# Loading FFN weights by column parts, halving a projection pass and turning held weight pieces on VectorE, in a fused kernel of memory attention and FFN

## The chip, the cores and the metric

The kernel runs on one core of a Trainium2 chip. The metric is the device time of one launch in microseconds. A time is the median over runs; the traces are of single executions.

## The reference

The input x has 2048 rows of 640. Attention goes through it in 64 segments of 32 rows; each segment sees 8 memory rows and its own rows, and its output for the memory rows is the next segment's memory. A feed-forward network (FFN) works on the same x, and a gate mixes the two.

```python
mem = mem0
for s in range(n_seg):                       # 64, one after the other
    xs = x[:, s * seg_len:(s + 1) * seg_len, :]
    h = jnp.concatenate([mem, xs], axis=1)   # 8 + 32 rows
    q = jnp.einsum('btd,dhe->bhte', h, Wq)   # 32 heads of 192; k and v alike
    ...
    scores = jnp.einsum('bhqe,bhke->bhqk', q, k) * scale
    scores = jnp.where(mask[None, None], scores, -1000000000.0)
    p = _softmax(scores, axis=-1)
    o = jnp.einsum('bhqk,bhke->bhqe', p, v)
    o = jnp.einsum('bhte,hed->btd', o, Wo)
    mem = o[:, :M, :].copy()
    outs.append(o[:, M:, :])
a = jnp.concatenate(outs, axis=1)
b = jnp.einsum('bsf,fd->bsd', _gelu(x @ w_gate) * (x @ w_up), w_down)   # 1536 inner columns
return g * a + (1 - g) * b                   # g = sigmoid((x * gate_w).sum(-1))
```

## The kernel before

The program is written as a list of operations. `_Sched.add` appends each to the stream of its engine and notes which regions of SBUF, PSUM and HBM it reads and writes; semaphore waits follow from these regions. Within an engine the order is the order of the calls, and a DMA belongs to the stream of the engine that issues it: SP issues the loads of weights and x, ACT the stores and the loads of scratch data (`AUXQ`). A wait stands in the stream, so it holds back all that comes behind it. Two operations that write one region keep their order, even when they touch different parts of it.

The work has three stages.

1. The FFN (`ffn_transposes`, `ffn_gu`, `ffn_down`), in four blocks of 512 rows. For each of 12 groups f of 128 inner columns, TensorE computes G (L782) and U (L785), each from five 128-row slices; ACT applies gelu (L788) and VectorE multiplies (L790). SP loads x's first block, `w_gate`, `w_up` (each 1920 KB in one DMA), x's second block and `w_down`, then pieces of the attention's weights.

2. The left pass (L844 to L871). "Left" names the 8 rows of every segment that don't fit beside the memory rows in a 32-row tile: 64 segments of 8, 512 columns (`XL`). Their Q and K need no memory, so they are computed ahead for all segments. An octant `o_` is 8 heads; for each of four octants and for Q and K there are 12 chunks of 128 output columns, each five matmuls of 128x512 (L852) into one PSUM bank, banks 0 to 7 in turn. Chunks are evicted by VectorE (L862) and ACT (L859) in turn, into one of two staging areas `lst`, and both name the whole area as the region they write. At the octant's end ACT issues four stores of 768 KB to HBM scratch (L867).

3. The segments (`segment`), by the hand-written order `PROG`: for each octant Q, K (`cmode`, L931; evicted L935), V and left V (L951), scores (L993), softmax, weighted sums (L1071), then Wo (L1094). VectorE copies the segment's memory rows (L1139), from which the next segment starts. Left Q/K of the segment come from scratch with `stg_load` (L907), left x with `xleft_load`.

The attention's weights are cut into 108 pieces of 384 or 320 KB. Most are resident in SBUF, 20 are streamed for every segment through a ring of five slots (L567), and two are held in unused parts of PSUM: `HELD2` (a piece of Wq) and `HELD` (a piece of Wo), which ACT copies to SBUF in each segment (`held2_copy`, L610, and `held_copy`, L623). Residents have three classes by their place. Class 0 is loaded at the start; class 2, above the staging areas, after the FFN (`load_residents(2)`); class 1, under `XL` and the staging areas, only when the left pass is done (`load_late`), at most `LATE` = 24 pieces ahead of use. The left pass needs streamed pieces too (`issue_left`, L635, through the same ring).

Between left pass and segments, `chain_init` transposes the first memory on TensorE (L728), ACT issues `x_load(0)` (L678), and ACT evicts the transposed memory into the same tile behind it (L732). `held_init` then brings the two held pieces into PSUM so that ACT's later copy is plain data: it loads a piece, transposes it by 128x128 blocks on TensorE (L882), copies it to SBUF on VectorE (L885) and transposes it back into its PSUM places (L896), first `HELD2`, then `HELD` through the same buffers.

Of the kernel before, what the change touches and what calls it, by code (L numbers as in the profile page):

```python
# [3 lines left out]
ACTF = mybir.ActivationFunctionType  # L4
# [217 lines left out]
def _build(nc, A_x, A_mem0, A_Wq, A_Wk, A_Wv, A_Wo, seg_len, w_gate, w_up, w_down,  # L222
           gate_w, out, opts=None):
    opts = dict(opts or {})
    Bsz, S, Dm = A_x.shape
    M = A_mem0.shape[1]
# [112 lines left out]
    def bview(o, nbytes, plo=0, phi=128):  # L339
        return arena[plo:phi, o // 2:(o + nbytes) // 2]  # L340
# [4 lines left out]
    def sreg(o, nbytes, plo=0, phi=128):  # L345
        return Rg("sb", o, o + nbytes, plo, phi)
# [71 lines left out]

    wg_sb = bview(ffn_off["wg"], KT * Df * 2).rearrange("p (k f) -> p k f", f=Df)
    wu_sb = bview(ffn_off["wu"], KT * Df * 2).rearrange("p (k f) -> p k f", f=Df)  # L420
    wd_sb = bview(ffn_off["wd"], FT * Dm * 2).rearrange("p (f n) -> p f n", n=Dm)
    r_wg = sreg(ffn_off["wg"], KT * Df * 2)
    r_wu = sreg(ffn_off["wu"], KT * Df * 2)
    r_wd = sreg(ffn_off["wd"], FT * Dm * 2)
# [12 lines left out]
    XLB = KT * NL * 2  # L437
    STB = NSEG * 2 * LW * 2
    o_XL = ffn_base - XLB
# [8 lines left out]
    def psb(bank):  # L448
        return ps[:, bank, :].bitcast(BF)
# [17 lines left out]
    def piece_size(key):  # L467
        return GO if key[0] == 3 else GQ
# [123 lines left out]
    late_done = [0]  # L592
    LATE = 24

# [55 lines left out]
    def load_residents(cls):  # L650
        for key in order:
            if key in res_off and slot_class[key] == cls:
                load_resident(key)
# [34 lines left out]
    ffn_x_load(0)  # L688
    S_.add("sp", lambda e: e.dma_start(wg_sb, w_gate.rearrange("(k p) f -> p k f", p=128)), writes=[r_wg], dma_sem="wg")
    S_.add("sp", lambda e: e.dma_start(wu_sb, w_up.rearrange("(k p) f -> p k f", p=128)), writes=[r_wu], dma_sem="wu")  # L690
    if NFB > 1:
# [33 lines left out]

    def chain_init():
        pv7 = psb(7)
        S_.add("pe", [lambda e, k=k: e.transpose(pv7[:, k * M:(k + 1) * M], mem0r[0:M, k * 128:(k + 1) * 128], ident[0:M, 0:M])  # L728
                      for k in range(KT)],
               reads=[r_mem0r, r_ident], writes=[r_ps[7]], name="mem0T")  # L730
        x_load(0)
        S_.add("act", lambda e: e.activation(out=Hb[0][:, :, 0:M], in_=pv7[:, 0:KT * M].rearrange("p (k m) -> p k m", m=M),  # L732
                                             func=ACTF.Copy),
               reads=[r_ps[7]], writes=[r_Hm[0]], name="mem0T evac")

# [43 lines left out]
    def ffn_gu(blk):  # L779
        for f in range(FT):  # L780
            gb = 3 + 2 * (f % 2)
            S_.add("pe", [lambda e, k=k, f=f, gb=gb: e.matmul(ps[:, gb, 0:FB].rearrange("p (s t) -> p s t", t=L), wg_sb[:, k, f * 128:(f + 1) * 128], xT_sb[:, k],  # L782
                                                              start=(k == 0), stop=(k == KT - 1)) for k in range(KT)],
                   reads=[r_wg] + r_xT, writes=[r_ps[gb]], name="ffn G %d %d" % (blk, f))
            S_.add("pe", [lambda e, k=k, f=f, gb=gb: e.matmul(ps[:, gb + 1, 0:FB].rearrange("p (s t) -> p s t", t=L), wu_sb[:, k, f * 128:(f + 1) * 128], xT_sb[:, k],  # L785
                                                              start=(k == 0), stop=(k == KT - 1)) for k in range(KT)],
                   reads=[r_wu] + r_xT, writes=[r_ps[gb + 1]], name="ffn U %d %d" % (blk, f))
            S_.add("act", lambda e, f=f, gb=gb: e.activation(out=gl_sb[f % 2], in_=ps[:, gb, 0:FB], func=ACTF.Gelu_apprx_tanh),  # L788
                   reads=[r_ps[gb]], writes=[r_gl[f % 2]], name="ffn gelu")
            S_.add("dve", lambda e, f=f, gb=gb: e.tensor_tensor(out=hT_sb[:, f, :], in0=ps[:, gb + 1, 0:FB], in1=gl_sb[f % 2], op=ALU.mult),  # L790
                   reads=[r_ps[gb + 1], r_gl[f % 2]], writes=[r_hT[f]], name="ffn h")
# [43 lines left out]
    S_.add("sp", lambda e: e.dma_start(mem0r[0:M, :], A_mem0[0]), writes=[r_mem0r], dma_sem="mem0")  # L835
    gate_spread()
    load_residents(2)
    for lo, hi in ((0, NG // 2), (NG // 2, NG)):
# [5 lines left out]
    for o_ in range(NOCT):  # L844
        st, rst_ = lst[o_ % 2], r_lst[o_ % 2]
        for m in range(2):
            gs = [left_piece((m, o_, k)) for k in range(KT)]
            for i in range(12):
                bk = nbk[0] % 8
                nbk[0] += 1  # L850
                c = i
                S_.add("pe", [lambda e, k=k, g_=gs[k][0], i=i, bk=bk: e.matmul(  # L852
                    ps[:, bk, 0:NL].rearrange("p (g t) -> p g t", t=L), g_[:, i * 128:(i + 1) * 128], XL[:, k], start=(k == 0), stop=(k == KT - 1))
                    for k in range(KT)], reads=[x[1] for x in gs] + [r_XL], writes=[r_ps[bk]],
                    name="left o%d m%d c%d" % (o_, m, i))
                dst = st[:, :, m].rearrange("p s (b r h) -> p s b r h", b=6, h=2)[:, :, c // 2, :, c % 2]
                src = ps[:, bk, 0:NL].rearrange("p (s i) -> p s i", i=M)
                if i % 2:
                    S_.add("act", lambda e, dst=dst, src=src: e.activation(out=dst, in_=src, func=ACTF.Copy),  # L859
                           reads=[r_ps[bk]], writes=[rst_], name="left evac")  # L860
                else:
                    S_.add("dve", lambda e, dst=dst, src=src: e.tensor_copy(out=dst, in_=src),  # L862
                           reads=[r_ps[bk]], writes=[rst_], name="left evac")
        nd = max(1, NSEG // 16)
        for d in range(nd):
            lo, hi = d * NSEG // nd, (d + 1) * NSEG // nd
            S_.add(AUXQ, lambda e, lo=lo, hi=hi, st=st, o_=o_: e.dma_start(  # L867
                qkl[lo:hi].rearrange("s p c -> p s c")[:, :, 2 * LW * o_:2 * LW * (o_ + 1)],
                st[:, lo:hi].rearrange("p s m c -> p s (m c)")),
                reads=[rst_], writes=[Rg("qk", 64 * o_ + lo, 64 * o_ + hi)], dma_sem="lst%d_%d" % (o_ % 2, d),  # L870
                name="left store")  # L871

    def held_init(key, parts):
        n = piece_size(key) // 2
        t1, r1 = bview(wsB_off["Q"], 2 * n), sreg(wsB_off["Q"], 2 * n)
        t2, r2 = bview(wsB_off["vl"], 2 * n), sreg(wsB_off["vl"], 2 * n)
        assert wsB_off["stg"] >= wsB_off["Q"] + 2 * n and n % 128 == 0
        dst = t1.rearrange("p (c n) -> p c n", n=Dm) if key[0] == 3 else t1
        S_.add("sp", lambda e: e.dma_start(dst, piece_src(key)), writes=[r1], dma_sem="held%d" % key[0], name="held load")
        for b, c0 in ((3, 0), (4, 8)):  # L880
            nb = min(8, n // 128 - c0)
            S_.add("pe", [lambda e, b=b, c=c, c0=c0: e.transpose(psb(b)[:, 128 * (c - c0):128 * (c - c0 + 1)],  # L882
                                                                 t1[:, 128 * c:128 * (c + 1)], ident)
                          for c in range(c0, c0 + nb)], reads=[r1, r_ident], writes=[r_ps[b]], name="heldT")
            S_.add("dve", lambda e, b=b, c0=c0, nb=nb: e.tensor_copy(out=t2[:, 128 * c0:128 * (c0 + nb)],  # L885
                                                                     in_=psb(b)[:, 0:128 * nb]),
                   reads=[r_ps[b]], writes=[r2], name="heldT evac")
        for b, c0, c1, p0 in parts:
            fns = []
            c = c0  # L890
            while c < c1:
                blk, lo = divmod(c, 128)
                hi = min(128, lo + c1 - c)
                if lo == 32:
                    hi = 64
                fns.append(lambda e, b=b, blk=blk, lo=lo, hi=hi, o=p0 + c - c0: e.transpose(  # L896
                    psb(b)[:, o:o + hi - lo], t2[lo:hi, 128 * blk:128 * (blk + 1)], ident[lo:hi, lo:hi]))
                c += hi - lo
            S_.add("pe", fns, reads=[r2, r_ident], writes=[r_ps[b]], name="heldTT")

    chain_init()
    issue_ring(0, B_RING - 1)
    held_init(HELD2, HB2)
    held_init(HELD, [(b, 256 * b, 256 * b + 256, 768) for b in range(5)])
    S_.add("pool", lambda e: e.memset(p_sb, 0.0), writes=[r_p])
# [352 lines left out]
```

## Time and profile before

| | |
|---|---|
| median of four runs | 1905.13 us (1892.21 to 1909.58) |
| the profiled execution | 1909.52 us, of which the span is 1907.7 |
| TensorE busy | 1757.6 us, 92% of the span |
| VectorE, ACT busy | 928.6 us (49%), 875.5 us (46%) |
| data moved | 550.98 MB, mean 289 GB/s |
| FFN | up to 183.15 us |
| left pass | 183.15 to 293.94 us |
| first scores | 325.93 us |
| end of segment 0 (L1139) | 354.38 us |
| mean granted TensorE clock | 0.983 |

Times in the profile are from the start of the span. A row of the timeline gives start, duration, engine, line, operation, output and input, number of instructions, and in brackets how long the engine had been idle and what released it. ACTq and SPq are the engines' sequencers while they issue DMAs. Busy time of TensorE contains pipelining, so a busy TensorE is not one at its peak.

### The profile page before, as it was taken

Reading aid. Unit: us, or ns where it says so; the run is one execution under the profiler, and the core shown is the slowest. Engines: PE = TensorE matmul, PEld = TensorE weight load, DVE = VectorE, ACT = ScalarE, POOL = GpSimd, SP = SyncE. Lnnn points to the kernel's source line nnn. Section 1 sums busy time; section 2 is a strip of 40 time slices with the busy share of each in tenths; the row PEclk is TensorE's granted clock in tenths of the full one; section 3 lists DMA queues with packets and bytes.
Section 4 is the critical chain, followed back from the end, with each engine's and each line's share of the span. In section 5 each row is a group of like instructions: output and inputs, shape, how many; then the busy total and the mean of one; then the engine's idle time right before and its main releaser. Section 6 shows DMA issues by size and latency. Waiting matters only on the chain.

```text
span 1907.7 us, 78857 instructions
## 1 busy us (share of the span) xinstructions
PE 1757.6 (92%) x34429; PEld 1128.2 (59%) x34429; DVE 928.6 (49%) x2890; ACT 875.5 (46%) x2045; POOL 145.1 (8%) x547
## 2 busy tenths in 40 slices
PE   7999995799999999999999999999999999899898
PEld 3454443566665666666666666666666566666565
DVE  3222322455555555555555555555555555555455
ACT  2222322355544554545555545454555554455444
POOL 1000000000000000000000100000000000000000
PEclk9999997999999999999999999999999999999999
DMA  9511567999999999999999999999999999999998
GB/s 372 197 35 33 151 171 226 331 317 306 312 312 310 318 317 297 329 313 324 313 323 316 338 309 325 299 328 306 325 313 332 305 323 310 311 316 310 296 313 272
DMA packets 280422, 550.98 MB, mean 289 GB/s; under 512 B 82434, under 2 KB 106506, under 8 KB 280074
## 3 DMA queue, kind: packets, MB, share of 16 engines
q1 hardware_dynamic: 201386, 506.45, 77.7%
q10 hardware_dynamic: 78688, 39.48, 7.5%
q8 instruction: 269, 4.41, 0.9%
q14 instruction: 79, 0.65, 0.1%
HBM read 524.69 MB, written 21.10 MB: 286 GB/s over the span
## 4 chain that ended last, share of the span: by engine, by line
PE 67%; DMA 23%; DVE 4%; ACTq 3%; ACT 1%; issue 1%; SPq 0%; DVEq 0%
PE ps L931 20%; DMA arena<-in_A_Wo_dram 13%; PE ps L951 11%; PE ps L1094 10%; PE ps L852 4%; PE ps L1071 4%; DMA arena<-in_A_Wv_dram 4%; DMA arena<-in_A_Wq_dram 3%; PE ps L993 3%; PE ps L785 3%; PE ps L782 3%; DMA arena<-in_A_Wk_dram 3%; ACTq L867 2%; PE ps L800 2%; PE ps L985 2%; PE ps L975 1%
## 5 line engine op out<-in xcount | busy, mean ns | idle before, releaser
L931 PE MATMUL ps<-arena 128*32 128x384 bf16 x10240 | 512.3, 332 | 32.9 <-DVE arena L1154 16.2
L1094 PE MATMUL ps<-arena 128*40 128x320 bf16 x6144 | 479.3, 299 | 38.2 <-DMA arena<-in_A_Wo_dram 34.1
L1094 PEld LDWEIGHTS ps<-arena 128*40 128x40 bf16 x6144 | 312.5, 99 | 139.2 <-DMA arena<-in_A_Wo_dram 69.2
L935 ACT ACTIVATE arena<-ps 128x384 bf16<-128x384 f32 x512 | 311.7, 609 | 148.1 <-PE ps L931 129.7
L931 PEld LDWEIGHTS ps<-arena 128*32 128x32 bf16 x10240 | 254.1, 97 | 174.9 <-DVE arena L1154 20.7
L951 PE MATMUL ps<-arena 128*32 128x384 bf16 x5800 | 294.3, 331 | 3.2 <-DMA arena<-in_A_Wv_dram 2.6
L941 DVE STREAM_TRANSPOSE arena<-arena 128x192 f32<-128x192 f32 x512 | 190.1, 371 | 118.5 <-ACT arena L935 118.2
L610 ACT ACTIVATE arena<-ps 128x576 bf16<-128x576 bf16 (+1 forms) x192 | 113.5, 591 | 243.1 <-PE ps L1094 240.1
L951 PEld LDWEIGHTS ps<-arena 128*32 128x32 bf16 x5800 | 147.3, 98 | 91.9 <-DMA arena<-in_A_Wv_dram 8.4
L962 ACT ACTIVATE arena<-ps 128x384 bf16<-128x384 f32 x256 | 125.8, 491 | 153.8 <-PE ps L951 74.7
L911 POOL COPY arena<-arena 128x96 bf16<-128x96 bf16 x256 | 68.4, 267 | 1553.9 <-PE ps L993 826.9
L1048 DVE TENSOR_TENSOR arena<-ps,arena 128x320 bf16<-128x320 bf16 x256 | 125.7, 491 | 110.6 <-PE ps L1045 108.3
L1020 ACT ACTIVATE ps<-ps 104x160 f32<-104x160 f32 x256 | 72.9, 285 | 176.0 <-DVE ps L1010 175.1
L1139 DVE CAST arena<-ps 104x320 bf16<-104x320 f32 x63 | 31.0, 492 | 237.1 <-PE ps L1094 237.1
L1071 PEld LDWEIGHTS ps<-arena 128*64 128x64 bf16 x3072 | 112.3, 125 | 55.7 <-DVE ps L1010 23.4
L1075 ACT ACTIVATE arena<-ps 128x320 bf16<-128x320 f32 x256 | 112.1, 438 | 70.9 <-PE ps L1071 69.0
L1071 PE MATMUL ps<-arena 128*64 128x160 bf16 (+1 forms) x3072 | 136.2, 222 | 4.8 <-ACT arena L623 3.3
L993 PE MATMUL ps<-arena 64*40 64x40 bf16 (+1 forms) x4096 | 119.7, 181 | 0.3 <-issue 0.2
L1008 DVE TENSOR_REDUCE arena<-ps 104x4 f32<-104x160 f32 x256 | 81.3, 317 | 71.7 <-PE ps L993 71.4
L852 PE MATMUL ps<-arena 128*128 128x512 bf16 x480 | 106.0, 383 | 4.0 <-ACT arena L859 4.0
L993 PEld LDWEIGHTS ps<-arena 64*40 64x40 bf16 (+1 forms) x4096 | 99.7, 96 | 9.3 <-issue 0.5
L1022 DVE TENSOR_REDUCE arena<-ps 104x4 f32<-104x160 f32 x256 | 82.5, 322 | 46.5 <-ACT ps L1020 27.1
(73 smaller groups left out, 1500.1 us busy)
## 6 DMA issues: line engine op xcount, KB each, us to landing
arena<-in_A_Wo_dram SPq DMA_DIRECT2D x528, 320.0 KB, 4.5
arena<-in_A_Wk_dram SPq DMA_DIRECT2D x340, 384.0 KB, 4.9
arena<-in_A_Wq_dram SPq DMA_DIRECT2D x277, 384.0 KB, 4.8
arena<-in_A_Wv_dram SPq DMA_DIRECT2D x209, 384.0 KB, 4.9
left_qk_scratch<-arena ACTq DMA_DIRECT2D x16, 768.0 KB, 8.1
arena<-left_qk_scratch ACTq DMA_DIRECT2D x64, 192.0 KB, 5.0
arena<-in_A_x_dram SPq DMA_DIRECT2D x4, 640.0 KB, 15.3
xt_scratch<-arena ACTq DMA_DIRECT2D x4, 640.0 KB, 9.0
```

Of the source, the lines that this page charges most:

```text
L610: S_.add("act", lambda e: e.activation(out=bview(o_held2, GQ)[:, c0:c1], in_=psb(b)[:, p0:p0 + c1 - c0], func=ACTF.Copy), reads=[r_ps[b]], ...
L852: S_.add("pe", [lambda e, k=k, g_=gs[k][0], i=i, bk=bk: e.matmul(ps[:, bk, 0:NL].rearrange("p (g t) -> p g t", t=L), g_[:, i * 128:(i + 1) ...
L931: S_.add("pe", [lambda e, j=j, k=k, gv=gv: e.matmul(ps[32 * j:32 * j + 32, bank, 0:384].rearrange("p (c i) -> p c i", i=32), Hb[hb][:, k, ...
L935: S_.add("act", lambda e: e.activation(out=rows_sb[m].rearrange("p (b i h) -> p b h i", b=6, h=2), in_=ps[:, bank, 0:384].rearrange("p (b ...
L941: S_.add("dve", lambda e: e.transpose(out=dst[:, :, 0:L], in_=rows_sb[m].bitcast(F32).rearrange("p (c r) -> p c r", r=L)), reads=[r_rows[m ...
L951: return [lambda e, j=j: e.matmul(ps[32 * j:32 * j + 32, bk, 0:384], lhs, g_[:, 384 * j:384 * (j + 1)], start=(k == 0), stop=(k == KT - 1) ...
L962: S_.add("act", lambda e: e.activation(out=v_sb[o % NVB], in_=ps[:, bank, 0:384], func=ACTF.Copy), reads=[r_ps[bank]], writes=[r_v[o % NVB ...
L993: fns.append(lambda e, gp=gp, lo=lo, hi=hi, b=(3 * tl + c) // 2, h=(3 * tl + c) % 2, tl=tl, last=(c != 1): e.matmul(ps[gp:gp + R, bank, tl ...
L1048: S_.add("dve", lambda e: e.tensor_tensor(out=PTm, in0=apx(pv[:, 0:104], [[64, 2], [0, 4], [1, R]]), in1=apx(mbd, [[0, 2], [1, 4], [0, R]] ...
L1071: fns.append(lambda e, lhs=lhs, left=left, h=h, dst=dst, rhs=rhs: e.matmul(dst, lhs, rhs, start=not left, stop=left, tile_position=(0, 64 ...
L1075: S_.add("act", lambda e: e.activation(out=apx(u[:, 0, 0, :], [[R, 2], [3 * R, 4], [1, R]]), in_=ps[:, A, 0:2 * W].rearrange("p (c t r) -> ...
L1094: fns.append(lambda e, g_=g_, i=i, c=c, h=h, tl=tl, cc=cc, u=u: e.matmul(ps[64 * h:64 * h + R, OB, 0:HD], u[:, tl, cc, :], g_[:, i, HD * h ...
```

## The change

The weights `w_gate` and `w_up` are loaded in two column parts each, 512 and 1024 columns, in the order gate, up, gate, up. Groups f = 0 to 3 name the first part as what they read, the others the second.

The left pass goes through each octant twice, with half of the columns each time (256, 32 segments). The chunks are five matmuls of 128x256, evicted as before into the staging area of that half, which is half as large; after each half ACT issues two stores of 768 KB. The residents lie in other places accordingly: 13 pieces are of class 1 instead of 21, and 14 of class 2 instead of 6. `LATE` is 64, so all late pieces are issued before the ring's sixth piece of segment 0.

`chain_init` now stands behind octant 0 and takes the next bank in turn. The held pieces are loaded by SP right after the FFN, before the class 2 residents, each into a buffer of its own. Behind octant 1, VectorE turns each in 32x32 blocks of 4-byte words (`held_turn`); after the left pass it turns them again, part by part, from SBUF into their PSUM places (`held_put`). Turning twice gives the original data. TensorE's transposes for it are gone.

```diff
+    FW = (512, Df - 512)
...
+    HS = NSEG // 2
+    STB = HS * 2 * LW * 2
...
-    LATE = 24
+    LATE = 64
...
+    for i in range(2):
+        for n, w in (("wg", w_gate), ("wu", w_up)):
+            S_.add("sp", lambda e, i=i, n=n, w=w: e.dma_start(
+                wgu_sb[n, i], w.rearrange("(k p) f -> p k f", p=128)[:, :, FW[0] * i:FW[0] * i + FW[i]]),
+                writes=[r_wgu[n, i]], dma_sem="%s%d" % (n, i))
...
+    held_buf = {HELD2: (wsB_off["Q"], wsB_off["vl"]), HELD: (wsB_off["uT"], wsB_off["stg"])}
...
+    def held_turn(key):
+        n = piece_size(key)
+        a_, b_ = held_buf[key]
+        S_.add("dve", lambda e: e.transpose(out=fview(b_, n), in_=fview(a_, n)), reads=[sreg(a_, n)], writes=[sreg(b_, n)],
+               name="held turn")
+
+    def held_put(key, parts):
...
+            S_.add("dve", lambda e, b=b, c0=c0, c1=c1, p0=p0: e.transpose(
+                out=ps[:, b, p0 // 2:(p0 + c1 - c0) // 2], in_=fview(b_, n)[:, c0 // 2:c1 // 2]),
+                reads=[sreg(b_, n)], writes=[r_ps[b]], name="held put")
...
+    held_load(HELD2)
+    held_load(HELD)
     load_residents(2)
...
     for o_ in range(NOCT):
-        st, rst_ = lst[o_ % 2], r_lst[o_ % 2]
-        for m in range(2):
-            gs = [left_piece((m, o_, k)) for k in range(KT)]
-            for i in range(12):
...
+        for hf in range(2):
+            st, rst_ = lst[hf], r_lst[hf]
+            for m in range(2):
+                gs = [left_piece((m, o_, k)) for k in range(KT)]
+                for i in range(12):
...
+                        ps[:, bk, 0:NL // 2].rearrange("p (g t) -> p g t", t=L), g_[:, i * 128:(i + 1) * 128],
+                        XL[:, k, NG // 2 * hf:NG // 2 * (hf + 1)], start=(k == 0), stop=(k == KT - 1))
...
+            for d in range(2):
+                lo, hi = d * HS // 2, (d + 1) * HS // 2
...
+        if o_ == 0:
+            chain_init(nbk[0] % 8)
+            nbk[0] += 1
+        if o_ == 1:
+            for key in (HELD2, HELD):
+                held_turn(key)
+
+    held_put(HELD, [(b, 256 * b, 256 * b + 256, 768) for b in (1, 2, 3, 4, 0)])
+    held_put(HELD2, HB2)
     issue_ring(0, B_RING - 1)
-    held_init(HELD2, HB2)
-    held_init(HELD, [(b, 256 * b, 256 * b + 256, 768) for b in range(5)])
```

## The prediction

> **What bounds the kernel now.** First the page's strip of 40 slices (47.7 us each).
>
> ```profile
> PE   7999995799999999999999999999999999899898
> DMA  9511567999999999999999999999999999999998
> ```
>
> From slice 8 on TensorE and DMA are both full: 62 of the 64 segments run evenly (VectorE's memory-row copy, L1139, at 354.38 for segment 0 and at 1880.6 for segment 62: 24.6 us each). The diff changes no instruction there, so only the first 355 us can move. The timeline of TensorE at the start:
>
> ```profile
> 10.55 1.86 PE L782 MATMUL ps<-arena 128*128 128x512 bf16 x4 [2.53 <-DMA arena<-in_B_w_gate_dram]
> 15.54 2.32 PE L785 MATMUL ps<-arena 128*128 128x512 bf16 x5 [2.70 <-DMA arena<-in_B_w_up_dram]
> ```
>
> TensorE waits for the last byte of each whole matrix. Next, the busy time of TensorE in the four octants of the left pass (stretch, length, busy, clock, DMA):
>
> ```profile
> 183.15:209.60 26.45, 26.45 (x125) 1.00 0.44 137
> 209.60:236.60 27.00, 25.83 (x121) 1.00 0.60 161
> 236.60:266.60 30.00, 27.80 (x122) 0.94 0.59 145
> 266.60:293.30 26.70, 25.88 (x120) 1.00 0.56 147
> ```
>
> and the timeline around one octant's end:
>
> ```profile
> 237.32 10.16 ACTq L867 DMA_DIRECT2D left_qk_scratch<-arena  x4
> 247.58 0.73 ACT L859 ACTIVATE arena<-ps 128x512 bf16<-128x512 f32 x1 [10.29 <-issue]
> 248.34 0.73 DVE L862 CAST arena<-ps 128x512 bf16<-128x512 f32 x1 [10.04 <-ACT arena L859]
> 248.36 1.86 PE L852 MATMUL ps<-arena 128*128 128x512 bf16 x5 [2.20 <-ACT arena L859]
> ```
>
> ACT issues four stores for 10 us; VectorE waits for ACT, because all evictions of an octant write one region and so alternate strictly; TensorE runs on until eight banks are full, then stops. The bound is therefore the chain of evictions: 24 per octant, 0.755 us from start to start when they are behind (249.10, 249.86, 250.61), and the stores' issue (9.2 us at 210.07). 23 x 0.755 + 9.2 = 26.6, against 27.0 measured for the second octant; TensorE alone needs 26.1. Last, TensorE between the passes and in segment 0:
>
> ```profile
> 294.00 0.28 PE L728 MATMUL ps<-arena 8*128 8x8 bf16 x5 [0.88 <-ACT arena L859]
> 298.08 1.46 PE L882 MATMUL ps<-arena 128*128 128x128 bf16 x12 [3.81 <-DMA arena<-in_A_Wq_dram]
> 315.79 0.50 PE L896 MATMUL ps<-arena 128*128 128x128 bf16 x3 [13.95 <-ACT arena L732]
> 325.93 0.47 PE L993 MATMUL ps<-arena 64*40 64x40 bf16 x16
> 336.21 0.83 PE L931 MATMUL ps<-arena 128*32 128x384 bf16 x16 [2.38 <-DMA arena<-in_A_Wq_dram]
> ```
>
> The held pieces wait for their load, then for a bank that mem0T's eviction on ACT holds, and that eviction waits for stores and x_load. The first scores come 32.0 us after the last eviction (293.94), segment 0's L1139 60.4 us after it. So: three stretches, summed on the profiled execution (span 1907.7, time 1909.52).
>
> **1. FFN weights in parts.** x lands at 5.6; whole w_gate, 1.97 MB, lands 4.9 us later: 400 GB/s. The parts of 0.66 MB take 1.6 us each, so they land at about 7.2 and 8.9; xT is evicted by 9.1 (the POOL copies that read it start at 9.10). G0 starts at 9.1 instead of 10.55, and U0 follows without the wait. From 15.54 three groups (U0, G1, U1) took 5.5 us, 4.7 of it at half pace, then 1.08 each. From 9.1, G0, U0 and a quarter of G1 run at half pace (4.8), 1.75 groups at 1.08 (1.9): G2 starts at 15.7 instead of 21.06. **-5.4**. The rest of the parts lands by about 15.5; f=4 needs it at 20. The two DMAs more on SP (0.5 us each) push back x's second block, which is needed at 38, and nothing nearer. The ACT stall at 49.13 (store issue, 6.2 us, behind x's scratch store) moves along; DMA stays full up to 69 in both.
>
> **2. Left pass in halves.** 960 matmuls of 256 columns for 480 of 512: same columns, 96 more groups at 0.013 us (five of 512 take 1.08 for 1.067): 26.1 x 4 + 1.3 = 105.7 us if the 480 further weight loads hide. Here a rule speaks against: the Trainium skill, "TensorE: Matmul & The Clock Gate", "Back-to-back issue gap", gives 81 ns for a 128-column pair of load and matmul in a stream, 25 more than the isolated 56. Rows: 20 transposes, each with its own weights, take 43.44 to 44.56, 56 ns each. At 25 ns more, a half (120) would take 15.8 instead of 13.1 and cost the sum some 15 us; I take the row.
>
> Evictions of 256 columns are not in the trace. Upper end: nothing saved, 0.755. Lower: on ACT the plain rows (160: 0.324, 320: 0.438, 512: 0.60) give 0.38 for 256, the scattered form 0.735 at 512 and 0.609 at 384 gives 0.07 to 0.11 more; DVE 0.725 at 512 and 0.322 at 160 gives 0.42 to 0.43. With 0.03 of handover one step is 0.455 to 0.49; I take 0.467, by these rows. A half then has 23 x 0.467 = 10.7 of evictions and the issue of two stores, 0.37 + 2.7 + 0.1 = 3.2: 13.9, over TensorE's 13.1. The chain of evictions stays the bound, 55.6 for four halves where two octants had 53 to 57: the halving itself brings nothing. Two boundaries cost more:
>
> - First half. SP now loads both held pieces (behind the b stores' landing) and 14 residents in place of 6, 6.1 MB, 15 us of DMA from about 7.5 us into the pass (first resident: +6.1). The stores start in the middle. Packets of SP's queue (q1) and ACT's (q10), in 4 us with both, then in 4 us with stores alone:
>
> ```profile
> q1 hardware_dynamic: 526, 1.43, 89.1%
> q10 hardware_dynamic: 524, 0.17, 16.4%
> ...
> q10 hardware_dynamic: 2955, 1.13, 113.2%
> ```
>
> One for one: 131 packets per us instead of 739. A following DMA was taken up when 750 (at 55.33) to 1044 (at 213.2) of the previous 2048 had gone: 5.7 to 8.0 us. With 6.6, ACT is back at +22.4 instead of +17: 5.4 lost. If bytes were shared evenly it would be 1 us.
> - After octant 0, mem0T's eviction on ACT waits for x_load, which lies in ACT's queue behind two stores: first packets 1.9 us after the issue (211.9 for 210.07), 4224 packets at 739 take 5.7, landing 1.2 later (the octant's last store: 224.3), the copy 0.2: 9.0 from the stores' start instead of 3.2, **5.8** lost. Behind it stand octant 1's ACT evictions, for them DVE's, for them TensorE's banks (mem0T takes one).
>
> Last eviction, counted from the pass's start: 13.8; 22.4 + 10.7 = 33.1; 42.1 + 10.7 = 52.8; then 13.9 each with 0.9 and 0.5 for SP's ring loads at the octants' ends: 66.7, 81.5, 95.4, 109.8, 123.7. Before: 110.8. **+12.9**. TensorE running cold after these stalls (3.8 us at 248.36) is covered by eight full banks. The two DVE turns (768 and 640 words; 192 take 0.371, so 1.8 to 2.7 in all) lie under the two stores' 3.2; uncovered they cost that. The stores' landing (8 us) is under the other half's 13.9.
>
> **3. Between the passes.** Gone: load, 45 transposes and four copies (L882 to L896), mem0T and x_load. Added: eight DVE puts into PSUM, about 3 us, under ACT's stores. What is late next: ACT still issues two stores, then stg_load waits for their landing; behind it are held2 copies and all row evictions, and Vl waits for the left x. SP at the same moment issues one ring piece and seven Wo (2.6 MB, 1408 packets, about 8 us), which slow the stores: 1200 packets gone by +9.2, the other 2900 at 739 by +13.1, landing +14.3. stg_load 3.0, POOL fills 0.6: scores at **+18** (before +32.0). With LATE 64, six more Wo wait on SP for the same landing, and the ring's sixth piece stands behind them: landed at about +22, when Q2 needs it at +21; that microsecond I leave to the range. Eight pieces (six of V, two of Wo) are now loaded during the left pass and leave this place, so the waits from 336 to 345 mostly go. Without waits the trace needs 20.7 from scores to L1139: **+38.7** against 60.4, **-21.8** (-18 to -26).
>
> **Sum:** -5.4 + 12.9 - 21.8 = -14.3: 1895.2 for the profiled execution. That one is 4.4 above the median, 1905.1 (four runs, 1892.2 to 1909.6); from the median: **1891**, 0.7% less.
>
> **Rivals.** (a) The stores are not held up: no loss at the first half (-5.4), final landing at +9 (-5): 1880.5. For it: the threshold for taking up the next DMA is known only within 750 to 1044, and the loads could be done sooner; against: one-for-one packets. (b) Segment 0 waits for streamed pieces behind the late Wo: L1139 at +47 instead of +38.7, 1899. For it: SP's order, 2.38 at 336.21; against: 13 late pieces where there were 21. (c) Ends slower: the eviction of 256 columns hardly shrinks, because a fixed cost dominates. Place: 184 evictions in the chain; price 184 us per us of step; from 0.544 on it decides. At 0.60 it is +24.5: 1915.5. For it: 512 against 384 columns on ACT saves only 0.13; against: slopes of three rows. (d) It does nothing: the parts' small rows and stalls eat all, 1905.
>
> **Numbers.** Main case 0.45 (own range 1883 to 1899), a 0.35, b 0.10, c 0.06, d 0.04. Faster by over 1% means under 1886 (1% is about what a measurement of this kernel can tell): nearly all of a and a fifth of the main case, 0.42; slower by over 1%, over 1924: half of c and little else, 0.04; within: 0.54. The range runs from a's lower side, 1875, to b's upper, 1903; under 2 in 10 is outside.
>
> **What would show it.** G2 at 15.7; evictions of 0.42 to 0.47 at steps of 0.47; half-passes of 14 us, the second near 19 and the third near 20; the last eviction about 124 after the pass's start; scores 18 and L1139 39 us after it. Wrong if evictions step above 0.54 or under 0.44, if ACT is back within 4 us at the first boundary, or if segment 0 waits for ring pieces.

## The result, and the profile after

The changed kernel takes 1891.75 us (median of 32 runs, 1883.76 to 1905.85), the kernel before 1906.06 (53 runs): a ratio of 0.9928, 95% interval 0.9914 to 0.9943. The forecast was 1891. The profiled execution has a span of 1895.1 us where the one before had 1907.7.

First the page's strip of 40 slices. It differs from the one before in slices 0 to 7; behind them TensorE and DMA are at eight tenths or more in both.

```profile
PE   8999796999999999999999999999999999999998
DMA  9512657999999999999999999999999999999998
```

VectorE's copy of segment 0's memory rows (now L1155) is at 341.78 instead of 354.38: 12.6 us earlier. The spans differ by the same 12.6, since 1553.3 us follow the copy in both traces. That they are equal is chance: over the fourteen traces of this document this rest takes 1540.5 to 1556.8 us, and 9 us less in one trace than in another of the same kernel ("halves without these two" below). What the change did must be read ahead of the copy. At the start (timeline of TensorE):

```profile
9.20 2.29 PE L794 MATMUL ps<-arena 128*128 128x512 bf16 x5 [1.09 <-DVE arena L774]
11.29 1.56 PE L797 MATMUL ps<-arena 128*128 128x512 bf16 x5
12.68 1.24 PE L794 MATMUL ps<-arena 128*128 128x512 bf16 x5
14.84 1.24 PE L794 MATMUL ps<-arena 128*128 128x512 bf16 x5
```

The waits of 2.53 and 2.70 for whole matrices are gone; the third G is at 14.84 (before 21.06). The left pass follows at 175.32 (183.15). In its first five stretches, from one issue of stores to the next (TensorE's windows: stretch, length, busy, clock, DMA share, GB/s):

```profile
175.32:189.68 14.36, 14.36 (x134) 1.00 0.73 218
189.68:209.52 19.84, 15.10 (x119) 0.83 0.86 294
209.52:230.96 21.44, 16.06 (x125) 0.84 0.39 94
230.96:244.56 13.60, 13.60 (x127) 1.00 0.63 176
244.56:259.69 15.13, 14.43 (x132) 1.00 0.59 156
```

The second and third are 5 to 8 us longer than the others: TensorE is idle for 4.7 and 5.4 us in them, and its clock falls. ACT's timeline says why:

```profile
189.68 7.95 ACTq L906 DMA_DIRECT2D left_qk_scratch<-arena  x2
209.52 3.65 ACTq L906 DMA_DIRECT2D left_qk_scratch<-arena  x2
213.19 2.61 ACTq L687 DMA_DIRECT2D arena<-xt_scratch  x1
218.19 0.20 ACT L744 ACTIVATE arena<-ps 128x40 bf16<-128x40 bf16 x1 [8.71 <-DMA arena<-xt_scratch]
301.19 6.04 ACTq L906 DMA_DIRECT2D left_qk_scratch<-arena  x2
```

Two stores take 7.95 us to issue while SP loads residents; later mem0T's eviction waits for segment 0's x behind the next two. Between the passes (TensorE, then SP):

```profile
314.78 3.38 PE L967 MATMUL ps<-arena 128*32 128x384 bf16 x37 [11.15 <-DMA arena<-left_xt_scratch]
319.52 0.46 PE L1009 MATMUL ps<-arena 64*40 64x40 bf16 x16
324.11 0.51 PE L947 MATMUL ps<-arena 128*32 128x384 bf16 x8 [1.09 <-DMA arena<-in_A_Wq_dram]
```

```profile
299.06 18.41 SPq L656 DMA_DIRECT2D arena<-in_A_Wo_dram  x13
```

The transposes are gone, and in their place TensorE waits 11.15 us for the left x, which ACT issues behind the last stores. The first scores come at 319.52 (325.93), and of the waits for streamed pieces 1.09 and 0.30 are left.

### The profile page after: what moved, and what is told of

It reads as the page before. It is cut to its first block, busy times and chain, and to the rows that moved or that the text cites. A ratio compares the mean times of both kernels' runs of the same rounds, so it can differ in the third digit from the quotient of the medians.

```text
span 1895.1 us, 79916 instructions
## 1 busy us (share of the span) xinstructions
PE 1757.4 (93%) x34864; PEld 1171.4 (62%) x34864; DVE 937.9 (49%) x2944; ACT 884.2 (47%) x2093; POOL 145.1 (8%) x547
## 4 chain that ended last, share of the span: by engine, by line
PE 67%; DMA 23%; DVE 5%; ACTq 2%; ACT 2%; issue 1%; SPq 0%; DVEq 0%
PE ps L947 20%; DMA arena<-in_A_Wo_dram 13%; PE ps L967 11%; PE ps L1110 10%; DMA arena<-in_A_Wq_dram 4%; PE ps L890 4%; DMA arena<-in_A_Wv_dram 4%; PE ps L1087 4%; PE ps L1009 3%; PE ps L794 3%; PE ps L797 3%; PE ps L812 2%; PE ps L1001 2%; DMA arena<-in_A_Wk_dram 2%; PE ps L991 1%; PE ps L1165 1%
## 5 line engine op out<-in xcount | busy, mean ns | idle before, releaser
L947 PE MATMUL ps<-arena 128*32 128x384 bf16 x10240 | 512.5, 332 | 27.8 <-DVE arena L1170 15.8
L1155 DVE CAST arena<-ps 104x320 bf16<-104x320 f32 x63 | 31.0, 492 | 233.6 <-PE ps L1110 233.6
L1087 PE MATMUL ps<-arena 128*64 128x64 bf16 (+1 forms) x3072 | 136.8, 222 | 6.3 <-ACT arena L632 3.6
L890 PE MATMUL ps<-arena 128*128 128x256 bf16 x960 | 111.1, 280 | 12.0 <-ACT arena L898 6.5
L1009 PE MATMUL ps<-arena 64*40 64x40 bf16 (+1 forms) x4096 | 120.3, 181 | 2.1 <-issue 1.9
L1024 DVE TENSOR_REDUCE arena<-ps 104x4 f32<-104x160 f32 x256 | 81.3, 318 | 75.8 <-PE ps L1009 75.7
L890 PEld LDWEIGHTS ps<-arena 128*128 128x128 bf16 x960 | 95.6, 100 | 27.2 <-ACT arena L898 7.6
L1009 PEld LDWEIGHTS ps<-arena 64*40 64x40 bf16 (+1 forms) x4096 | 100.3, 96 | 11.3 <-issue 2.6
```

Source lines behind the costliest of these rows:

```text
L890: S_.add("pe", [lambda e, k=k, g_=gs[k][0], i=i, bk=bk, hf=hf: e.matmul(ps[:, bk, 0:NL // 2].rearrange("p (g t) -> p g t", t=L), g_[:, i * ...
L947: S_.add("pe", [lambda e, j=j, k=k, gv=gv: e.matmul(ps[32 * j:32 * j + 32, bank, 0:384].rearrange("p (c i) -> p c i", i=32), Hb[hb][:, k, ...
L1009: fns.append(lambda e, gp=gp, lo=lo, hi=hi, b=(3 * tl + c) // 2, h=(3 * tl + c) % 2, tl=tl, last=(c != 1): e.matmul(ps[gp:gp + R, bank, tl ...
L1087: fns.append(lambda e, lhs=lhs, left=left, h=h, dst=dst, rhs=rhs: e.matmul(dst, lhs, rhs, start=not left, stop=left, tile_position=(0, 64 ...
```

## The experiments

All times of this table are of one profiled execution each, in us. "Pass" is from the left pass's first matmul to the issue of its last stores, "scores" and "copy" from there to the first scores and to segment 0's memory-row copy. The ratio is to the kernel before, over all runs of both that were measured together.

| kernel | pass starts | pass | scores | copy | copy lies at | ratio, 95% interval |
|---|---|---|---|---|---|---|
| before | 183.15 | 110.8 | 32.0 | 60.4 | 354.4 | 1 |
| changed | 175.32 | 125.9 | 18.3 | 40.6 | 341.8 | 0.9928 (0.9914 to 0.9943) |
| changed, once more | 177.85 | 124.3 | 18.5 | 40.9 | 343.1 | 0.9944 (0.9918 to 0.9970) |
| parts alone | 178.03 | 109.3 | 32.6 | 61.6 | 348.9 | 0.9973 (0.9950 to 0.9996) |
| held and mem0T alone | 182.22 | 117.0 | 29.3 | 55.5 | 354.8 | 1.0032 (1.0014 to 1.0050) |
| halves without these two | 176.15 | 119.7 | 19.8 | 41.4 | 337.2 | 0.9890 (0.9855 to 0.9926) |
| the same, once more | 176.23 | 120.1 | 20.0 | 41.8 | 338.1 | 0.9895 (0.9864 to 0.9927) |
| held on TensorE | 175.90 | 123.6 | 19.4 | 41.3 | 340.8 | 0.9934 (0.9908 to 0.9959) |
| LATE 24 | 176.46 | 123.4 | 17.7 | 44.4 | 344.2 | 0.9940 (0.9918 to 0.9961) |
| x earlier | 178.18 | 114.5 | 18.8 | 40.3 | 333.0 | 0.9873 (0.9824 to 0.9921) |
| two regions | 175.86 | 121.3 | 20.1 | 42.2 | 339.4 | 0.9934 (0.9911 to 0.9957) |
| residents spread | 176.51 | 120.3 | 18.5 | 42.2 | 339.1 | 0.9904 (0.9875 to 0.9933) |
| all three | 176.25 | 114.2 | 15.6 | 43.2 | 333.6 | 0.9893 (0.9862 to 0.9924) |
| all three, SP's order | 175.28 | 114.3 | 18.4 | 42.2 | 331.8 | 0.9874 (0.9831 to 0.9917) |

The place of the copy says what the time will be: its shift against the kernel before, divided by 1905, lies inside the interval in every row but one ("held and mem0T alone", 0.4 us later and 0.3% slower; why is open). That holds for medians; the span of a single trace differs more, by the rest behind the copy.

**The parts of the change, one at a time.**

Parts alone: in the kernel before,

```diff
-    S_.add("sp", lambda e: e.dma_start(wg_sb, w_gate.rearrange("(k p) f -> p k f", p=128)), writes=[r_wg], dma_sem="wg")
-    S_.add("sp", lambda e: e.dma_start(wu_sb, w_up.rearrange("(k p) f -> p k f", p=128)), writes=[r_wu], dma_sem="wu")
+    for i in range(2):
+        for n, w in (("wg", w_gate), ("wu", w_up)):
+            S_.add("sp", lambda e, i=i, n=n, w=w: e.dma_start(
...
```

> The kernel before with only the FFN weights in column parts. Theory (each of the three stretches has its own price, and the price of one is carried to the end): the left pass starts at about 175.3 instead of 183.15, takes 111 as before, and the memory-row copy of segment 0 lies at 346.5 instead of 354.38; the time falls by 8, ratio 0.996. Rival (the weights' DMA is the bound behind the start, so that what is won at the start is waited for again): the left pass still starts early, but the copy lies at 350 or later and the time falls by 0 to 4, ratio 0.998 to 1.000.

The pass starts 5.1 us earlier, the copy lies 5.5 earlier, and the time falls by 0.27% or 5 us. The theory's point holds: what is won at the start is still there at the copy. Its size, 8, was one trace's good start (below), and the 5 lies between it and the rival's 0 to 4.

Held and mem0T alone: in the kernel before, `held_load`, `held_turn`, `held_put` and `chain_init(nbk[0] % 8)` as in the change, with whole octants.

> The kernel before with only the held pieces loaded early and turned by VectorE, and mem0T behind octant 0; whole octants, whole weight matrices. Theory (the early loads of eight more pieces and the short last stores, which the halves bring, carry about half of the gain between the passes): left pass about 117 (mem0T's eviction waits for the x load behind four stores), first scores +24 after its last eviction, memory-row copy of segment 0 at +52, near 352; time -2, ratio 0.999. Rival (the held work itself was the whole cost between the passes): scores at +18 and the copy at +39, near 339; time -15, ratio 0.992.

The rival falls: 4.9 us are won between the passes and 6.2 lost in the left pass. The theory was right about the pass (117.0) and too hopeful by 3.5 behind it. With the transposes gone, TensorE waits instead; ACT's timeline and TensorE's:

```profile
299.25 18.82 ACTq L893 DMA_DIRECT2D left_qk_scratch<-arena  x4
```

```profile
323.82 3.07 PE L954 MATMUL ps<-arena 128*32 128x384 bf16 x36 [23.47 <-DMA arena<-left_xt_scratch]
```

Four stores hold ACT for 18.8 us, the left x is issued behind them, and the held work had lain in that wait.

Held on TensorE: in the changed kernel

```diff
-    held_load(HELD2)
-    held_load(HELD)
...
+    held_init(HELD2, HB2)
+    held_init(HELD, [(b, 256 * b, 256 * b + 256, 768) for b in range(5)])
```

> The changed kernel with the held pieces brought in as before (loaded behind the left pass, transposed on TensorE, copied by VectorE), all else as changed. Theory (in the changed kernel the stores' landing and the left x set the first scores, and TensorE waits 11 us for them, so that the held work would fit into this wait): scores at +20 after the last eviction where the changed kernel has +18.4, the copy of segment 0 at +43 instead of +40.6; time +2 against the changed kernel, ratio to before 0.994. Rival (the held work is what the old way cost): scores at +27 or later, the copy at +49 or later; time +8 or more against the changed kernel, ratio 0.997 or more.

The theory holds, on its better side. Between the passes the old way costs 0.4 to 0.7 us more; in the left pass it saves 0.7 to 2.3, since its loads no longer stand ahead of the first stores (their issue takes 6.65 us, not 7.95). In sum it is 0.3 to 1.5 us ahead of the change, which the ratios cannot tell apart.

Halves without these two: the same edit, and mem0T behind the left pass as well.

```diff
-        if o_ == 0:
-            chain_init(nbk[0] % 8)
-            nbk[0] += 1
...
+    chain_init(7)
     issue_ring(0, B_RING - 1)
```

> The changed kernel with mem0T, its x load and the held work behind the left pass as in the kernel before; column parts, halves, places of the residents and LATE as changed. Theory (between the passes two stores instead of four and thirteen late pieces instead of twenty-one are most of the gain; the held work and mem0T are worth some 5): left pass 120 (the mem0T boundary's 6 is saved), copy of segment 0 at +46 after its last eviction, so at 342 to 344, time within 3 of the changed kernel, ratio to before 0.993. Rival (the held work and mem0T behind the left pass are what cost between the passes, as with the kernel before): TensorE again waits about 14 for mem0T's eviction, copy at +55 or later, near 352, time +9 against the changed kernel, ratio 0.998.

The theory holds and more: the copy is 4.6 us ahead of the changed kernel's. ACT and TensorE between the passes:

```profile
295.84 2.50 ACTq L880 DMA_DIRECT2D left_qk_scratch<-arena  x2
306.24 0.20 ACT L744 ACTIVATE arena<-ps 128x40 bf16<-128x40 bf16 x1 [10.43 <-DMA arena<-xt_scratch]
```

```profile
306.50 0.50 PE L909 MATMUL ps<-arena 128*128 128x128 bf16 x3 [5.22 <-ACT arena L744]
315.66 0.46 PE L1006 MATMUL ps<-arena 64*40 64x40 bf16 x16
```

The wait for mem0T's eviction, 13.95 in the kernel before, is 5.22 although nothing of the held work was changed: the last stores take 2.5 us to issue instead of 14.04. Since the result spoke against two parts of the change, both kernels were run again on one chip.

> The changed kernel itself once more, beside the next run, to tell what differs from one execution to the next from what differs between kernels. Theory (the stages up to the memory-row copy of segment 0 repeat within 2 us; what varies lies in the FFN's start and in the segments): left pass 124 to 127, the copy at +39 to +42 after it, at 341 to 344. Rival (the stages themselves scatter by 4 or more, so that the differences of single traces among the experiments carry no weight): left pass or transition off by 4 or more.

> The changed kernel with mem0T, its x load and the held work behind the left pass, once more, on the chip of the run of the changed kernel. Theory (the two moves cost the left pass some 6 us and give back little between the passes): left pass 119 to 121, copy at +40 to +43, at 336 to 339, 4 us ahead of the changed kernel; ratio to before 0.990, under that of the changed kernel. Rival (the first trace was a favourable one): copy within 2 us of the changed kernel's, ratio equal or above.

Pass and what follows it repeat within 1.6 us in both pairs of traces (the starts within 2.6); the copy is 5.1 us earlier without the two parts, and the medians are 1881.52 (6 runs) and 1889.35 (12 runs).

LATE 24: one number changed.

```diff
-    LATE = 64
+    LATE = 24
```

> The changed kernel with LATE 24 instead of 64: seven late Wo pieces stand ahead of the streamed pieces of segment 0 on SP instead of thirteen. Theory (the six more cost a little by standing ahead of the Q pieces): SP's row of late Wo falls from 18.4 to about 15, the Q wait of 1.09 and the V wait of 0.30 go, the copy of segment 0 comes 1 to 1.5 us earlier. Rival (DMA is full there and the bytes are the same): the six pieces wait at another place, the copy moves by less than 0.5 or comes later.

The rival is right: the copy comes at +44.4. TensorE waits 0.68 for Q, 2.13 for K, 0.55 for V: on SP the thirteen late pieces now stand in groups of two to four among the streamed ones, which come late. Behind the pass LATE 64 is worth 3.5 to 3.8 us; counted from the pass's start it is 1.3 to 2.5, since this trace's pass was shorter, and the ratios (0.9940, and 0.9928 and 0.9944) show no difference.

**The waits that are left.**

x earlier: in the changed kernel

```diff
-        x_load(0)
         S_.add("act", lambda e: e.activation(out=Hb[0][:, :, 0:M], ...
...
+    x_load(0)
     nbk = [0]
     for o_ in range(NOCT):
```

> The changed kernel with the load of segment 0's x issued on ACT ahead of the left pass instead of behind octant 0's stores. Theory (mem0T's eviction waits for this load, and all evictions of octant 1 for it): ACT's idle time of 8.7 us ahead of mem0T's eviction falls to under 1, the last eviction comes 5 us earlier (120.5 after the pass's start instead of 125.9), the copy of segment 0 likewise; time -5 against the changed kernel, ratio to before 0.990. Rival (the load has only changed its place: issued among SP's weight loads it holds ACT back at the pass's start as long): the last eviction moves by less than 2.

ACT's timeline, and TensorE in the two stretches that had been long:

```profile
193.26 4.38 ACTq L906 DMA_DIRECT2D left_qk_scratch<-arena  x2
211.51 0.20 ACT L743 ACTIVATE arena<-ps 128x40 bf16<-128x40 bf16 x1 [2.32 <-PE ps L890]
```

```profile
193.26:209.22 15.96, 14.06 (x132) 1.00 1.07 363
209.22:222.87 13.65, 12.63 (x116) 1.00 0.45 121
```

The theory holds: mem0T's eviction no longer waits for DMA, and its stretch falls from 21.44 to 13.65. That is 7.8, not the 5 awaited: besides the wait, TensorE's clock stays at 1.00 where it had been at 0.84. That the first stores now issue in 4.38 us was not expected, and takes 3.9 more off the pass.

Two regions: in the changed kernel

```diff
-    r_lst = [sreg(ffn_base + b * STB, STB) for b in range(2)]
+    r_lst = [[sreg(ffn_base + b * STB + i * STB // 2, STB // 2) for i in range(2)] for b in range(2)]
...
-                    if i % 2:
+                    if i // 2 % 2:
...
-                               reads=[r_ps[bk]], writes=[rst_], name="left evac")
+                               reads=[r_ps[bk]], writes=[rst_[i // 2 % 2]], name="left evac")
```

> The changed kernel with each staging area named as two regions, one written by VectorE alone and one by ACT alone (the engines change every second chunk), so that neither waits for the other's eviction; the stores read both. Theory (strict turns of ACT and VectorE at 0.483 us per eviction bound a half): evictions run two at a time at 0.44 to 0.46 each, VectorE goes on while ACT issues stores, a half falls to TensorE's 13.1, the left pass from 125.9 to about 119; time -7, ratio to before 0.989. Rival (TensorE with 256 columns per weight load is the bound): the left pass moves by less than 2.

TensorE in three undisturbed halves:

```profile
244.56:257.77 13.21, 13.21 (x122) 1.00 0.71 180
257.77:270.87 13.10, 13.10 (x122) 1.00 0.57 151
270.87:283.97 13.10, 13.10 (x122) 1.00 0.62 151
```

The halves do fall to TensorE's 13.1 us, so turns in the evictions were what bound them in the changed kernel. But the two long stretches stay (20.0 and 21.8 us), so the pass wins 3.1 to 4.6 and not 7; of that 1.5 goes again between the passes, and the ratio shows no gain: inconclusive for the time.

Residents spread: seven of the fourteen loads behind the streamed pieces of octant 1.

```diff
-    load_residents(2)
+    class2 = [key for key in order if slot_class.get(key) == 2]
+    for key in class2[:7]:
+        load_resident(key)
...
+                if (o_, hf, m) == (1, 0, 1):
+                    for key in class2[7:]:
+                        load_resident(key)
```

> The changed kernel with seven of the fourteen residents that it loads at the pass's start loaded later, behind the streamed pieces of octant 1. Theory (the packets of SP's loads go one for one with those of ACT's stores): ACT's issue row at the first boundary falls from 7.95 to about 3.2 us, the last eviction comes 4 to 5 us earlier; time -4.5, ratio to before 0.990. Rival (the loads meet other stores instead): the first row falls, another boundary's row grows by 3 or more, and the last eviction moves by less than 2.

The first row falls to 4.41 us, the pass by 4.0 to 5.5, no other row grows by 3: the theory holds for the pass. Between the passes 1.5 are given back.

All three together, with `xleft_load(0)` moved behind octant 0:

> The changed kernel with the earlier x load, the two regions per staging area and the spread residents together, and with the first left x loaded behind octant 0 instead of at the end. Theory (the three waits lie one behind another and add): left pass about 109, first scores +15 after it, copy of segment 0 near 322; time -18 against the changed kernel, ratio to before 0.983. Rival (one bound hides another: TensorE or DMA takes over): left pass above 115, time -8 or less.

The rival comes out for the time: by the ratios some 7 us under the changed kernel, not 18. The pass, 114.2, is just under the rival's 115 and no shorter than with x earlier alone (114.5). TensorE is busy with it for 108.0 us, and most of the rest is one wait. ACT's timeline:

```profile
203.60 5.07 ACTq L911 DMA_DIRECT2D left_qk_scratch<-arena  x2
208.77 3.27 ACTq L687 DMA_DIRECT2D arena<-left_xt_scratch  x1
212.14 0.20 ACT L743 ACTIVATE arena<-ps 128x40 bf16<-128x40 bf16 x1 [8.62 <-issue]
```

The load of the left x was put where the x load had been, between octant 0's stores and mem0T's eviction. ACT is at its issue for 3.27 us behind 5.07 for the stores, TensorE waits 5.29 for the eviction, and this stretch takes 21.26 us at a clock of 0.84, as in the changed kernel (21.44), where x earlier had 13.65. So this kernel does not show that the three waits don't add; a version with the left x loaded ahead of the pass was not run. And the copy is at +43.2 though the scores are at +15.6; TensorE and SP:

```profile
315.07 0.51 PE L953 MATMUL ps<-arena 128*32 128x384 bf16 x8 [3.98 <-DMA arena<-in_A_Wq_dram]
```

```profile
290.23 17.47 SPq L656 DMA_DIRECT2D arena<-in_A_Wo_dram  x13
```

The sixth streamed piece, a Q, stands behind thirteen late pieces that wait for the last stores to land. So SP's order was tried, with ACT and TensorE below:

```diff
-        if seg == 0:
+        if seg == 0 and issued.get(0, 0) > B_RING + 1:
             load_late(oi + LATE)
```

> The kernel with all three waits removed (and the left x loaded early), and on SP the sixth and seventh streamed piece of segment 0 issued ahead of the thirteen late residents instead of behind them. Theory (there SP holds the sixth piece back behind late residents that wait for the last stores to land, while DMA stands idle for about 3 us): TensorE's wait of 3.98 for the Q piece goes, the copy of segment 0 comes 4 earlier, +39 after the last eviction, near 329.5; time -4 against that kernel, ratio to before 0.987. Rival (the late residents are then late themselves, or DMA is full): a wait of 3 or more appears at Wo or V, the copy stays at +42 or later.

```profile
294.15 8.21 ACTq L929 DMA_DIRECT2D arena<-left_qk_scratch  x1
```

```profile
304.72 0.82 PE L953 MATMUL ps<-arena 128*32 128x384 bf16 x5 [11.74 <-ACT arena L619]
```

The Q wait goes, as the theory says, and three of the four us come back elsewhere (the wait at mem0T's eviction stays, 8.85 us of ACT): ACT now needs 8.21 us to issue `stg_load` (4.91 before), held2's copy waits behind it, and TensorE for that. The copy is at +42.2. Neither theory foresaw this place. Of the versions with a ratio under 0.99, none can be told from another; "x earlier" has one edit against the changed kernel and a copy at 333.0.

## Why the prediction was right

The forecast sum was -14.3 us for the profiled execution; the changed kernel's two traces give -12.6 and -11.3 at the copy, and the medians of 53 and 32 runs -14.3. In the first trace each of the three terms is off by 2.0 to 2.4 us, the first for the better and the other two for the worse. The terms are about right in size, the third not for the reason named; that the sum comes this close is in part luck.

1. **Start.** Right: -5.4 predicted, -7.8 and -5.3 in the changed kernel's two traces. The first is a favourable draw in two places. TensorE ran at half pace for some 3 us at its start, in "parts alone" until 14.8, so the third G comes at 14.84 in one trace and at 15.61 in the other. And in all fourteen traces TensorE stalls for 1.5 to 2.7 us some 50 to 56 us into the span. Its clock over the 12 us from there is 0.86 in five of them, both with whole matrices among these, and the left pass starts 127.0 to 127.1 us after the stall; in the other nine it is 1.00, and 125.1 to 125.5. Like with like, the three traces with parts and 0.86 start the pass at 178.0 on the mean, 4.7 to 5.1 earlier than whole matrices (182.22 and 183.15). Why the clock stays up in some executions is open.

2. **Left pass.** +12.9 predicted, +15.1 and +13.5 measured. One eviction takes 455 ns on ACT and 442 on VectorE, a step 0.483 (predicted 0.467). The two boundaries were named and priced: 19.84 and 21.44 us for stretches predicted at 19.3 and 19.7. What was missing in the second is the clock: the text let eight full banks cover a cold TensorE, but the stretch has 16.06 us of busy TensorE at 0.84 for work that takes 13.1 to 13.6 warm. The row was the right choice against the rule: each of the three halves above has 120 matmuls of 256 columns, each with its own weights, in 13.1 us, 109 ns apiece, so the weight loads hide. The Trainium skill, "TensorE: Matmul & The Clock Gate", "Back-to-back issue gap", has a formula for a single one isolated that comes to 109 at 256 columns, and for sustained streams a surcharge at 128 columns (81 for 56) which no half here shows. (25 ns on 109 would have made a half 16.1 us, not the 15.8 of the prediction; nothing rests on it.)

3. **Between the passes.** -21.8 predicted (60.4 less 38.7 is 21.7), -19.8 and -19.5 measured. The size is nearly right, the step under it was not: the list "Gone: load, 45 transposes and four copies, mem0T and x_load" is not where the time came from. From the pass's start to the copy:

| | old held work, mem0T at the end | new held work, mem0T behind octant 0 |
|---|---|---|
| whole octants | 171.2, 170.9 | 172.5 |
| halves | 161.0, 161.8 | 166.5, 165.3 |

The halves bring 9.7 us, with their places of the residents and LATE 64; the two moves cost 1.5 with octants and 4.4 with halves. Of the 4.4, mem0T behind octant 0 is 3.5 (161.4 to 164.9, the one trace with held on TensorE), the held work the rest. The prediction had both sides of this in its text, 5.8 lost at mem0T's boundary and the scores set by two stores and what waits for them, but did not subtract them: once the end of the pass waits for stores and left x, taking transposes and mem0T out of that wait brings 0.8 us (copies at +40.6 and +40.9 against +41.4 and +41.8), and each us that is spent for it in the pass is lost. The sentence on what is late next was right: stores, stg_load and left x. How much of the 9.7 is the two stores and how much are thirteen late pieces instead of twenty-one was not separated; LATE is 1.3 to 2.5 of the sum from the pass's start, as far as one trace of "LATE 24" tells.

The rivals: (a), that the stores are not held up, is refuted by 7.95 us, and "residents spread" shows what it would have brought in the pass, 4.0 to 5.5 where 5.4 was named. (b), waits for streamed pieces behind late Wo, is 1.4 us in the changed kernel: the sign named for it, that segment 0 waits for ring pieces, did show, but small. With the scores earlier it grew to 3.98. (c) needed steps of 0.544. (d) is excluded by the interval.

## What to carry to other kernels

Before taking work out of a wait, ask what else the wait is for: the held transposes ran while stores drained, and their removal only made the wait visible. Price an early start and a late gain in one sum, since a load or a copy moved forward costs at its new place even where it was free at the old one (mem0T 3.5 us; the left x, put ahead of mem0T's eviction, brought back a wait that had just been removed). And where a kernel ends in an even stretch, one time stamp at its entrance compares variants more sharply than whole runs: the copy told 5 us apart in two pairs of traces, where the rest behind it varied by up to 16 us.

## What was not expected of the hardware

How many packets of a store have gone does not tell when the next store is taken up. In the changed kernel the second store was taken up 7.55 us after the first's issue, with 524 of the first's 2048 packets gone; with x earlier after 3.9 us with some 60 gone, under the same loads. So the threshold of 750 to 1044 packets of the prediction is no threshold; what sets it stays open.

A stall of 5 us of TensorE costs more than itself here: against the fourth stretch (13.60, all busy) the third lost 7.8 us, 5.4 idle and 2.5 in matmuls at a granted clock of 0.84. A stall of 1.5 to 2.7 us in the FFN was followed by 0.86 in five traces and by 1.00 in nine, at a price of some 1.8 us.
